# Zero matmuls and doubled scores in the opening of a fused attention and MLP kernel

## The chip, the cores and the metric

The kernel runs on one core of one Trainium2 chip. The metric is the device time of one execution in microseconds (us), as the median of several runs; lower is better. Five engines run their own instruction queues in order and meet at semaphores: TensorE (matmuls and weight loads), VectorE, ScalarE, GpSimd (here also issuing transfers) and SyncE (issuing transfers). A profile is one execution recorded by the hardware profiler, with times counted from the start of its span.

## What is computed

The inputs are q, k and v of 8 batches, 12 heads, 448 positions and 64 numbers per head, and two weight matrices (768 x 2048 and 2048 x 768), all float32. In the reference:

```
scores = (1/sqrt(64)) * q @ k^T              # per batch and head
attn   = max(scores, 0)**2 / 448
x      = attn @ v                            # rearranged to 3584 tokens x 768
h      = x @ w_in
g      = h * sigmoid(1.702 * h)
out    = g @ w_out                           # 3584 x 768, float32
```

There is no softmax, so scores need no row maximum or sum: each tile of scores is cut at zero, squared and multiplied with v.

## The kernel before

**Units.** The attention is cut into 24 units ("quads"), each four heads of one batch, three units to a batch. In a unit the 448 positions are taken as 7 blocks of 64. For each block j the function `scores` (L136) issues four matmuls of 64 x 64 weights by 448 columns, one in each quarter of the array, into one tile `sc` of two memory banks of the accumulator. `relu2` (L150) cuts a tile at zero into `rl` (float16), on ScalarE (L157) or, for a few, on VectorE (L154); a multiplication of `rl` with itself on VectorE then gives `at` (L171 and, here, out of a list of pending ones). When all seven blocks of a unit have their squares, `av_mm` (L174) multiplies them with v in 28 matmuls, and `xt_evac` copies the result to `xt`, the transposed input of the MLP.

**Buffers.** Score tiles share three buffers (`ps_s`), also used by the value products of all units but the first; a score therefore waits for the relu of the score three tiles earlier. All other products share two buffers (`ps_m`). There are three `rl` tiles, so a relu waits for the square three tiles earlier.

**The opening.** Before anything has been loaded, eight matmuls of a tile of zeros with itself (`zero`, L490 to L494) run into a scratch bank. The q and k of units 0 to 5 are loaded with a conversion to float16 by GpSimd's queue and transposed on TensorE: `trans_pe` (L124) issues 14 transposes into one bank, and VectorE copies them to kT or qT (L133). Those of units 6 to 23 are loaded by SyncE's queue, cast (`cast`, L96) and transposed by the transfer engines (`trans`, L107).

**Order.** Everything up to unit 8 and the first two groups of MLP columns is issued in an order written out by hand, a string of words (L521 to L536). `s2.3` is the score of unit 2, block 3 (with `d`: relu on VectorE; with `h`: relu held until the next MLP step), `k3` and `q3` are transposes, `a1` the value product of unit 1 with its copy, `f` and `F` steps of the first MLP product for groups 0 and 1, `m` and `n` of the second, `l` a bundle of loads, `L`, `W`, `K`, `Q`, `R` loads, casts and transposes of later units, other capitals sums of weights. In the kernel before, `e2` squares pending tiles, oldest first, until two are left. As engines keep the order in which they are given their work, a word sets what it is queued behind. After the words a loop mixes MLP steps and visits to the remaining units; after each visit `prefetch` (L599) brings up loads, casts and transposes of later units.

Of the kernel before, what the change touches and what calls it, by code (L numbers as in the profile page):

```python
# [8 lines left out]
F32 = mybir.dt.float32  # L9
F16 = mybir.dt.float16  # L10
AF = mybir.ActivationFunctionType
ALU = mybir.AluOpType
# [3 lines left out]
def kernel(  # L16
# [9 lines left out]
    nc = tc.nc  # L26
# [3 lines left out]
    J = S // 64  # L30
    NP = H // 4
    NU = B * NP
# [26 lines left out]
    ps_s = ctx.enter_context(tc.tile_pool(name="ps_s", bufs=3, space=bass.MemoryType.PSUM))  # L59
# [14 lines left out]
    def quad(t, b, pr):  # L74
        return t[b].rearrange("(a i s) (p j) d -> i (s p) a (j d)", a=2, i=NP, j=J)[pr]

    def load_qk(u):
        b, pr = divmod(u, NP)
        st = units.setdefault(u, {})
        for n, t in (("k", k), ("q", q)):  # L80
            x = stp.tile([128, 2, S], F32, name=f"{n}st", tag=f"{n}st")
            nc.sync.dma_start(
                out=x,
                in_=quad(t, b, pr))
            st[n] = x

    def load_v(u):
        b, pr = divmod(u, NP)
        st = units.setdefault(u, {})
        x = v16p.tile([128, 2, S], F16, name="v16", tag="v16")  # L90
        nc.gpsimd.dma_start(  # L91
            out=x,
            in_=quad(v, b, pr))
        st["v16"] = x
# [20 lines left out]
    def load16(u, n):  # L115
        b, pr = divmod(u, NP)
        st = units.setdefault(u, {})
        x = c16.tile([128, 2, J, D], F16, name=f"{n}16", tag=f"{n}16")
        nc.gpsimd.dma_start(
            out=x,  # L120
            in_=quad({"k": k, "q": q}[n], b, pr))
        st[n + "16"] = x
# [10 lines left out]
        nc.vector.tensor_copy(out=t, in_=ps[:, 0:J * 128])  # L133
        st[n + "T"] = t

    def scores(u, j):  # L136
        st = units[u]
        sc = ps_s.tile([128, 2, 512], F32, name="sc", tag="sc")
        for s in range(2):
            for a in range(2):  # L140
                r = slice(64 * a, 64 * a + 64)
                c = slice(64 * s, 64 * s + 64)
                nc.tensor.matmul(  # L143
                    out=sc[c, a, 0:S],
                    lhsT=st["kT"][r, j, c],
                    rhs=st["qT"][r, :, c],
                    start=True, stop=True)
        return sc

    def relu2(u, j, sc, dve=False):  # L150
        rl = rlp.tile([128, 2, S], F16, name="rl", tag="rl")
        at = atp.tile([128, 2, S], F16, name="at", tag="at")
        if dve:
            nc.vector.tensor_scalar(out=rl, in0=sc[:, :, 0:S], scalar1=0.0, scalar2=None,  # L154
                                    op0=ALU.max)
        else:
            nc.scalar.activation(out=rl, in_=sc[:, :, 0:S], func=AF.Relu)  # L157
        if defer[0]:
            pend.append((at, rl))
        else:  # L160
            nc.vector.tensor_tensor(out=at, in0=rl, in1=rl, op=ALU.mult)
        return at


    defer = [False]
    pend = []

    def flush(n=99):
        while pend and n:
            at, rl = pend.pop(0)  # L170
            nc.vector.tensor_tensor(out=at, in0=rl, in1=rl, op=ALU.mult)  # L171
            n -= 1

# [52 lines left out]
    ats = {}  # L226
# [115 lines left out]
    def weight_sum(o, x, y, op, i, eng):  # L342
        c = slice(2 * i, 2 * i + 2)
        eng.tensor_tensor(out=o[:, c, :], in0=x[:, c, :], in1=y[:, c, :], op=op)
# [110 lines left out]
    def w1(i):  # L455
        for a in range(2):
            nc.gpsimd.dma_start(
                out=win[i][64 * a:64 * a + 64, :, :],
                in_=w_rows[a, :, :, i * WQ * 128:(i + 1) * WQ * 128])
# [26 lines left out]
    with tc.manual_schedule():  # L486
# [3 lines left out]
        zero = gfp.tile([128, 1024], F16, name="zero", tag="gf")  # L490
# [19 lines left out]
        for n in ("k", "q"):  # L510
# [8 lines left out]

        defer[0] = True  # L520
        words = (  # L521
            "e2 e1 s0.0 s0.1 e0 q1 s0.2 e1 s0.3 s0.4 k1 e2 e2 s0.5 k2 e0 e0 s0.6 s1.0 a0m "
            "s1.1 e0 s1.2 e0 q2 s1.3 l0 e1 s1.4 s1.5 e2 s1.6 e1 e1 l1 s2.0 s2.1 e1 e1 e0 e1 "
            "a1 e0 k3 s2.2 s2.3 e1 e0 q3 s2.4 s2.5 e2 e3 e2 e1 s2.6 e1 s3.0 l2 e1 l3 e3 e0 a2 "
            "k4 s3.1 f0 s3.2 e2 e1 e0 e0 s3.3d f1 e1 s3.4h e2 e0 l4 s3.5 f2 q4 e1 e0 e2 f3 e1 "
            "f4 e0 e2 s3.6d e3 e1 e0 s4.0 k5 f5 G1 e2 s4.1 e1 e1 e0 e1 e0 e2 a3 e2 s4.2 f6 e1 "
            "e2 e0 e0 e0 s4.3d e1 e3 e0 l5 s4.4 e2 e1 q5 e2 s4.5d e0 f7 e0 e2 f8 s4.6 s5.0 f9 "
            "s5.1 a4 e2 e2 s5.2 e2 e1 e0 e0 f10 e0 e2 s5.3d e3 l6 f11 f12 L6 L7 f13 e3 s5.4 "
            "e2 s5.5 s5.6h e1 e2 f14 f15 Q6 e2 K6 R6 e1 a5 e0 e3 e0 L8 e2 m2 e2 m1 e2 F0 B2 "
            "W6 A2 C2 Q7 e1 K7 B1 F1 e1 C0 m0 e3 A1 B3 A0 F2 s6.0d e1 A3 B0 e0 e2 s6.1 R7 K8 "  # L530
            "s6.2h e0 e1 F3 e2 s6.3 W7 e0 L9 e1 s6.4h Q8 e2 F4 e3 e0 e2 C3 W8 e2 F5 R8 L10 E3 "
            "K9 s6.5 e0 s6.6 n0 e3 F6 W9 e1 s7.0d e0 s7.1 e2 E2 e2 e0 e2 F7 s7.2 e2 e2 a6 "
            "s7.3 C1 s7.4d F8 F9 e1 W10 e2 e0 Q9 F10 s7.5d e2 e2 e1 e3 s7.6h e3 e2 e2 e1 s8.0 "
            "e2 R9 e2 e3 e0 n1 e3 s8.1 s8.2 e1 a7 K10 E1 e1 e2 L11 s8.3 e1 E0 e2 e3 e2 F11 n2 "
            "e0 s8.4 e3 e1 e0 e0 e3 s8.5 D0 s8.6h e0 e0 Q10 W11 e2 e0 e0 e1 e2 F12 R10 e2 F13 "
            "D2 e3 e0 e0 e2 F14 D3 e1 D1 e0 F15 e1 W12 e0 e0 L12").split()  # L536
        loads = {"0": lambda: (load16(4, "k"), load16(4, "q"), load_v(4), w1(2)),
                 "1": lambda: (load16(5, "k"), load16(5, "q"), load_v(5)),
                 "2": lambda: w1(3),
# [2 lines left out]
        for w in words:  # L542
            t, w = w[0], w[1:]
            if t == "s":
                where = w[-1] if w[-1] in "dh" else ""
                u, j = (int(x) for x in w.rstrip("dh").split("."))
                sc = scores(u, j)
                if where == "h":
                    held.append((u, j, sc))
                else:  # L550
                    ats[u, j] = relu2(u, j, sc, where == "d")
            elif t in "kq":
                trans_pe(int(w), t)
            elif t == "a":
                u = int(w.rstrip("m"))
                if w[-1] == "m":
                    units[u]["av"] = [ps_m.tile([128, 512], F32, name="avm", tag="mm")
                                      for _ in range(2)]
                while any(p[0] is ats[u, jj] for p in pend for jj in range(J)):
                    flush(1)  # L560
                for jj in range(J):
                    av_mm(u, jj, ats.pop((u, jj)))
                xt_evac(u)
                done_units[0] = u + 1
            elif t == "f":
                m1(0, int(w))
            elif t == "F":
                m1(1, int(w))
            elif t in "mn":
                m2(0, int(w), int(t == "n"))  # L570
            elif t in "BACED":
                o, x, y, op = {"B": (w_b, wout[1][0], wout[1][1], ALU.subtract),
                               "A": (w_a, wout[0][0], wout[1][1], ALU.add),
                               "C": (w_c, wout[0][1], wout[0][0], ALU.subtract),
                               "E": (w_e, wout[0][1], wout[1][1], ALU.add),
                               "D": (w_d, wout[1][0], wout[0][0], ALU.add)}[t]
                weight_sum(o, x, y, op, int(w), nc.vector)
            elif t == "G":
                sp_gate(wout[0][int(w)][0:1, 0, 0:64])
            elif t == "L":  # L580
                load_qk(int(w))
            elif t == "W":
                load_v(int(w))
            elif t == "K":
                cast(int(w), "k", nc.scalar)
            elif t == "Q":
                cast(int(w), "q", nc.gpsimd)
            elif t == "R":
                trans(int(w))
            elif t == "e":  # L590
                flush(max(0, len(pend) - int(w)))
            elif t == "l":
                loads[w]()
        defer[0] = False

        loaded = [2 * NP + 7]
        prepped = [2 * NP + 5]

        def prefetch(upto_load, upto_prep):  # L599
            while loaded[0] < min(NU, upto_load):  # L600
                load_qk(loaded[0])
                load_v(loaded[0])
                loaded[0] += 1
            while prepped[0] < min(NU, upto_prep):
                cast(prepped[0], "k", nc.scalar)
                cast(prepped[0], "q", nc.gpsimd)
                trans(prepped[0])
                prepped[0] += 1

        def step_visit():  # L610
            visit4(visits.pop(0))
# [68 lines left out]
```

## Time and profile before

The time is 394.42 us, the median of three runs (393.89 to 394.83). The profiled execution has a span of 393.0 us and a mean granted TensorE clock of 0.984 of full.

| first 60 us in the profile before | us |
|---|---|
| TensorE busy | 51.04 |
| VectorE busy | 42.16 |
| ScalarE busy | 40.18 |
| GpSimd busy | 31.10 |
| mean TensorE clock | 0.91 of full |
| moved by transfers | 198 GB/s |

A "clock" in the profile is the rate that the hardware granted TensorE, as a share of full speed. "Busy" is the time in which an engine had an instruction under way; matmuls overlap one another, and their ends are modelled. "Idle before" a group is the time that the engine waited for something, and the arrow names what ended the wait. In the order of time, a line holds the start, the length, the engine, the source line, the operation and how many instructions were merged. The chain that ended last is followed back from the last instruction, at each step to whatever released it.

### The profile page before, as it was taken

What the parts mean: (1) busy time and instruction counts of PE and PEld (TensorE: products, weight loads), DVE (VectorE), ACT (ScalarE), POOL (GpSimd) and SP (SyncE); (2) the same over time, 40 slices, a digit from 0 to 9 for tenths busy, and PEclk for the clock granted to TensorE, in tenths of its full rate; (3) what the DMA queues carried; (4) which work ended last, traced back from release to release, by engine and by line L of the source; (5) the groups of instructions that cost most, each with busy time, mean ns of one, the idle gap of its engine ahead of it and who ended that gap; (6) DMA issues with size and microseconds to landing.
All of it is one profiled execution on the core that took longest, in us unless ns stands there. A gap on an engine that the chain in (4) does not pass through costs nothing.

```text
span 393.0 us, 7814 instructions
## 1 busy us (share of the span) xinstructions
PE 374.2 (95%) x3104; PEld 193.5 (49%) x3104; DVE 251.9 (64%) x408; ACT 226.2 (58%) x329; POOL 139.5 (35%) x200
## 2 busy tenths in 40 slices
PE   6869999999999999999999999999999999999993
PEld 2435455444455555444455555445444555554552
DVE  2788965899667675577476768275676667123473
ACT  3777673676676765776675656767675662242200
POOL 8444342644543432242442423342332221232100
PEclk9789999999999999999999999999999999999998
DMA  8999999999955929753397928667342301110333
GB/s 119 197 204 205 191 270 211 191 216 116 251 104 170 189 39 231 178 116 76 71 212 129 175 72 209 166 131 111 39 100 39 82 0 42 40 43 0 81 82 81
DMA packets 65221, 50.85 MB, mean 129 GB/s; under 512 B 35744, under 2 KB 61728, under 8 KB 65184
## 3 DMA queue, kind: packets, MB, share of 16 engines
q1 hardware_dynamic: 47872, 35.70, 39.4%
q0 software_dynamic: 17152, 14.55, 25.4%
q8 instruction: 24, 0.39, 0.4%
q10 hardware_dynamic: 160, 0.10, 0.1%
q14 instruction: 13, 0.11, 0.1%
HBM read 45.61 MB, written 11.01 MB: 144 GB/s over the span
## 4 chain that ended last, share of the span: by engine, by line
PE 78%; DVE 7%; ACT 7%; issue 4%; DMA 2%; POOL 1%; ACTq 0%; POOLq 0%
PE ht L292 32%; PE op L359 26%; PE sc L143 8%; PE av L183 7%; PE op L320 4%; ACT rl L157 4%; DVE osb L370 3%; DVE at L171 2%; DMA q<-in_q_dram 1%; ACT k L102 1%; ACT gf L297 1%; PE tr L129 1%; DMA out_dram<-osb 1%; DVE xt L203 0%; ACT eb L368 0%
## 5 line engine op out<-in xcount | busy, mean ns | idle before, releaser
L157 ACT ACTIVATE rl<-sc 128x896 f16<-128x896 f32 x159 | 140.7, 921 | 41.0 <-PE sc L143 40.0
L292 PE MATMUL ht<-xt,win 128*128 128x384 f16 (+1 forms) x768 | 160.8, 353 | 1.8 <-ACT gf L297 1.3
L299 POOL TENSOR_SCALAR gt<-gf 128x384 f16<-128x384 f32 (+1 forms) x128 | 86.1, 673 | 209.2 <-ACT gf L297 208.4
L171 DVE TENSOR_TENSOR at<-rl 128x896 f16<-128x896 f16 x168 | 113.2, 698 | 22.3 <-ACT rl L157 22.0
L297 ACT ACTIVATE gf<-ht 128x384 f32<-128x384 f32 (+1 forms) x128 | 70.1, 548 | 93.4 <-PE ht L292 84.3
L292 PEld LDWEIGHTS <-win 128*128 128x128 f16 x768 | 72.0, 98 | 76.8 <-issue 15.8
L359 PEld LDWEIGHTS <-gt 128*128 128x128 f16 x408 | 39.0, 98 | 32.1 <-issue 6.0
L143 PE MATMUL sc<-qT,kT 64*64 64x448 f16 x672 | 49.7, 366 | 3.8 <-ACT rl L157 2.3
L359 PEld LDWEIGHTS <-as 128*128 128x128 f16 x312 | 30.0, 98 | 23.7 <-issue 3.9
L359 PE MATMUL op<-wsum,gt 128*128 128x384 f16 x224 | 40.7, 326 | 0.5 <-ACT ea L368 0.4
L359 PE MATMUL op<-wout,as 128*128 128x384 f16 x224 | 40.7, 326 | 0.3
L370 DVE SCALAR_TENSOR_TENSOR osb<-op,osb 128x384 f32<-128x384 f32 (+1 forms) x45 | 23.6, 545 | 27.1 <-PE op L359 26.9
L203 DVE CAST xt<-av 128x896 f16<-128x896 f32 (+2 forms) x34 | 25.8, 785 | 19.2 <-PE av L183 19.2
L183 PE MATMUL av<-at,v 64*64 64x448 f16 x644 | 36.2, 359 | 0.7 <-ACT rl L157 0.4
L359 PE MATMUL op<-wout,gt 128*128 128x384 f16 (+1 forms) x184 | 32.4, 319 | 1.6 <-DVE osb L370 0.9
L143 PEld LDWEIGHTS <-kT 64*64 64x64 f16 x672 | 17.2, 106 | 29.4 <-issue 22.3
L370 DVE SCALAR_TENSOR_TENSOR osb<-op,ea 128x384 f32<-128x384 f32 x22 | 12.1, 552 | 24.7 <-PE op L359 13.4
L183 PEld LDWEIGHTS <-v 64*64 64x64 f16 x672 | 20.9, 110 | 14.0 <-issue 3.9
L354 DVE TENSOR_TENSOR as<-gt 128x1024 f16<-128x1024 f16 x36 | 27.1, 779 | 0.0
L91 POOL DMA_DIRECT2D v<-in_v_dram x24 | 17.9, 746 | 9.0 <-PE sc L143 5.2
L104 POOL CAST q<-qst 128x896 f16<-128x896 f32 x18 | 17.2, 954 | 0.3
L102 ACT ACTIVATE k<-kst 128x896 f16<-128x896 f32 x18 | 17.2, 958 | 0.0
(36 smaller groups left out, 158.7 us busy)
## 6 DMA issues: line engine op xcount, KB each, us to landing
out_dram<-osb SPq DMA_DIRECT2D x54, 192.0 KB, 3.0
kst<-in_k_dram SPq DMA_DIRECT2D x18, 448.0 KB, 4.6
qst<-in_q_dram SPq DMA_DIRECT2D x18, 448.0 KB, 5.8
v<-in_v_dram POOLq DMA_DIRECT2D x24, 224.0 KB, 4.5
win<-in_moe_w_in_dram POOLq DMA_DIRECT2D x8, 384.0 KB, 11.9
wout<-in_moe_w_out_dram POOLq DMA_DIRECT2D x4, 768.0 KB, 11.8
k<-in_k_dram POOLq DMA_DIRECT2D x6, 224.0 KB, 8.9
q<-in_q_dram POOLq DMA_DIRECT2D x6, 224.0 KB, 8.9
```

The costliest lines, as they stand in the source:

```text
L102: eng.activation(out=o, in_=i, func=AF.Copy)
L143: nc.tensor.matmul(out=sc[c, a, 0:S], lhsT=st["kT"][r, j, c], rhs=st["qT"][r, :, c], start=True, stop=True)
L157: nc.scalar.activation(out=rl, in_=sc[:, :, 0:S], func=AF.Relu)
L171: nc.vector.tensor_tensor(out=at, in0=rl, in1=rl, op=ALU.mult)
L183: nc.tensor.matmul(out=st["av"][s][64 * a:64 * a + 64, 0:S], lhsT=st["v16"][r, a, 64 * j:64 * j + 64], rhs=at[r, a, :], start=(j == 0), st ...
L203: nc.vector.tensor_copy(out=xts[g][:, 2 * pr:2 * pr + 2, c], in_=st["pair"][:, :, f])
L292: nc.tensor.matmul(out=ht[:, 0:n], lhsT=w[:, kk, fo:fo + 128], rhs=xts[g][:, kk, 0:n], start=(kk == 0), stop=(kk == NK - 1))
L297: nc.scalar.activation(out=gf[:, 0:n], in_=ht[:, 0:n], func=AF.Gelu_apprx_sigmoid, scale=1.0 / SC)
L299: nc.gpsimd.tensor_scalar(out=gts[g][:, f, 0:n], in0=gf[:, 0:n], scalar1=SC, scalar2=1.0, op0=ALU.mult, op1=ALU.mult)
L354: nc.vector.tensor_tensor(out=out_, in0=x, in1=y, op=op)
L359: nc.tensor.matmul(out=op[:, 0:cw], lhsT=lhs[:, f, :], rhs=w[:, f, c0:c0 + cw], start=(start and f == 0), stop=(stop and f == HF - 1))
L370: nc.vector.scalar_tensor_tensor(out=o, in0=op[:, 0:w], scalar=sc, in1=add, op0=ALU.mult, op1=ALU.add)
```

## The change

Three things are added and one is moved.

- A word `z3` issues three matmuls of zeros (128 x 128 by 512 columns) into a score tile taken from its pool ahead of time; the next score then uses that tile. It stands once ahead of `s0.0`, the first score, and once after `q1`, ahead of `s0.2`.
- A flag `t` on a score word issues the four matmuls of the score twice, with the same result. It stands on `s2.0` to `s2.5`, the first six scores of the third quad.
- In `prefetch` the casts and transposes of a unit are issued ahead of the loads of a later one, not after them.
- The words `e` that counted pending squares are replaced by words `x` that name them (`x2.3`); pending squares are kept by name. The order of the squares among the other words is the same.

What the zeros and the doubled scores are for is TensorE's activity: they give it work without use in places where it would wait, so that its clock may stay up. The order of the other instructions on TensorE is unchanged.

```diff
-    def scores(u, j):
+    early = []
+
+    def scores(u, j, times=1):
         st = units[u]
-        sc = ps_s.tile([128, 2, 512], F32, name="sc", tag="sc")
-        for s in range(2):
+        sc = early.pop() if early else ps_s.tile([128, 2, 512], F32, name="sc", tag="sc")
+        for s in [0, 1] * times:
             for a in range(2):
...
-            "e2 e1 s0.0 s0.1 e0 q1 s0.2 e1 s0.3 s0.4 k1 e2 e2 s0.5 k2 e0 e0 s0.6 s1.0 a0m "
...
+            "z3 s0.0 s0.1 x0.0 x0.1 q1 z3 s0.2 s0.3 s0.4 k1 x0.2 s0.5 k2 x0.3 x0.4 x0.5 s0.6 "
+            "s1.0 x0.6 a0m s1.1 x1.0 x1.1 s1.2 x1.2 q2 s1.3 l0 s1.4 s1.5 x1.3 s1.6 x1.4 x1.5 "
+            "l1 s2.0t s2.1t x1.6 x2.0 x2.1 a1 k3 s2.2t s2.3t x2.2 x2.3 q3 s2.4t s2.5t x2.4 "
+            "s2.6 x2.5 s3.0 l2 x2.6 l3 x3.0 a2 k4 s3.1 f0 s3.2 x3.1 x3.2 s3.3d f1 s3.4h x3.3 "
...
-                sc = scores(u, j)
-                if where == "h":
+                sc = scores(u, j, 2 if "t" in where else 1)
+                if "h" in where:
...
-            elif t == "e":
-                flush(max(0, len(pend) - int(w)))
+            elif t == "x":
+                at, rl = pend.pop(tuple(int(x) for x in w.split(".")))
+                nc.vector.tensor_tensor(out=at, in0=rl, in1=rl, op=ALU.mult)
+            elif t == "z":
+                early.append(ps_s.tile([128, 2, 512], F32, name="sc", tag="sc"))
+                for _ in range(int(w)):
+                    nc.tensor.matmul(out=early[0][:, 0, :], lhsT=zero[:, 0:128],
+                                     rhs=zero[:, 0:512], start=True, stop=True)
...
         def prefetch(upto_load, upto_prep):
-            while loaded[0] < min(NU, upto_load):
-                load_qk(loaded[0])
-                load_v(loaded[0])
-                loaded[0] += 1
             while prepped[0] < min(NU, upto_prep):
                 cast(prepped[0], "k", nc.scalar)
                 cast(prepped[0], "q", nc.gpsimd)
                 trans(prepped[0])
                 prepped[0] += 1
+            while loaded[0] < min(NU, upto_load):
+                load_qk(loaded[0])
+                load_v(loaded[0])
+                loaded[0] += 1
```

## The prediction

> **What bounds the kernel now.** I read the page first, then the chain that ended last, then TensorE's order of time in the first 33 us, then a table of stretches cut where the clock changes.
>
> ```profile
> PE 374.2 (95%) x3104; PEld 193.5 (49%) x3104; DVE 251.9 (64%) x408; ACT 226.2 (58%) x329; POOL 139.5 (35%) x200
> ...
> PEclk9789999999999999999999999999999999999998
> ```
>
> TensorE is busy 95% of the span, and its clock is below full in only three places: slices 2 and 3 (10 to 29 us), and the end. From 60 to 360 us it idles 3.7 us in 300 (busy 59.55, 59.49, 58.90, 59.08 and 59.24 of 60 us each), and none of its waits there is for a transfer. A saving at the start should therefore move everything after it. The start is where TensorE is not full: 51.04 of the first 60 us. The chain there, in order of time:
>
> ```profile
> 4.12 5.05 DMA q<-in_q_dram
> 9.17 0.04 issue
> 9.21 0.96 PE tr L129 x14
> 10.17 1.26 PE sc L143 x11
> 11.44 0.89 PE tr L129 x14
> 12.32 0.52 PE sc L143 x4
> 12.84 0.91 PE tr L129 x14
> 13.75 0.02 issue
> 13.77 0.62 DVE kT L133
> 14.40 2.21 DVE at L171 x4
> ...
> 22.71 2.85 PE av L183 x28
> ```
>
> So the chain runs through TensorE from 9.21 to 13.75, then VectorE and ScalarE, then TensorE again in 22.71 to 25.56. Both TensorE pieces run at half clock:
>
> ```profile
> 5.10:8.51 3.41, 1.74 (x36) 1.08 (x36) 1.25 (x2) 0.41 (x1) 3.41 (x6) 1.00 1.22 184
> 8.51:11.92 3.41, 2.71 (x38) 1.64 (x40) 1.78 (x3) 2.49 (x4) 2.59 (x4) 0.50 1.18 180
> 11.92:15.33 3.41, 3.41 (x46) 1.95 (x46) 2.72 (x5) 2.58 (x4) 2.14 (x4) 0.50 1.25 201
> 15.33:18.75 3.42, 2.20 (x46) 1.15 (x38) 2.95 (x8) 2.89 (x4) 0.92 (x2) 1.00 1.24 197
> 18.75:22.16 3.41, 1.92 (x31) 0.84 (x27) 3.17 (x7) 3.10 (x5) 1.88 (x3) 1.00 1.25 201
> 22.16:25.57 3.41, 2.98 (x34) 1.44 (x31) 2.22 (x4) 2.12 (x3) 1.37 (x2) 0.50 1.24 205
> 25.57:28.99 3.42, 2.60 (x48) 1.27 (x48) 3.10 (x6) 2.54 (x4) 1.41 (x2) 1.00 1.27 205
> ```
>
> The first column after the length is TensorE's busy time, the last but two its clock. The clock changes only at multiples of 3.41 us[...]. At full clock, 1.74 and 1.92 us of busy time (51% and 56%) were followed by half; 2.20 and 2.60 us (64%, 76%) were not. At half clock 2.71 us (79%) was not enough to come back; 3.41 and 2.98 us (100%, 87%) were.
>
> [...] 25.57 to 28.99 keeps its clock with only 1.51 us (44%) without its transposes (1.09), while 18.75 to 22.16 loses it with 1.72 us (1.92 less 0.20). I go by total busy time. [...] (weight loads of the warm-up on zeros start 0.43 us apart: 2.05, 2.48, 2.90); no row here shows 512 columns at full clock[...].
>
> **The change, part by part.**
>
> *Zeros before the first scores.* [...] They follow the transposes of q0, issued by 6.88; s0.0 starts at 7.67 after 0.72 us of waiting for the copy of qT. They need only the zero tile and an unused score buffer. They end near 7.55: hidden, cost 0 (at most 0.1). In the window 5.10 to 8.51 busy time goes from 1.74 to 2.39 us (70%), above the 64% that kept its clock: no fall at 8.51.
>
> *Zeros after the transposes of q1.* By the instruction order they stand behind those transposes, ahead of s0.2, not in the 0.97 us in which the transposes wait for q1. So 0.65 us lies on the chain if the clock is full, 3 x 0.427 = 1.28 us if it is half. Queued behind them are s0.2 to s0.4, for which ScalarE already waits 0.92 us at 10.74. Their use is the window 8.51 to 11.92: at full clock the real work in it shrinks to about 1.85 us (54%, a fall at 11.92); with zeros it is 2.5 us (73%).
>
> *The first half-clock stretch, walked forward.* q1 lands at 9.19 (issued 4.12, 5.1 to landing) in both kernels. Transposes at full clock take 0.52 to the next instruction (18.36 to 18.88), zeros 0.65: s0.2 starts at 10.36 against 10.10, its relu at 10.79 (0.43 after the score, as 8.10 after 7.67) against 10.74. Nothing is won so far. Relus follow at 0.81 (4.97 us for six). Three score groups of 0.19 end at 10.94, transposes of k1 at 11.46; s0.5 needs the buffer of s0.2's relu, 11.75; transposes of k2 (landed 5.54 + 6.3 = 11.84) from 11.94 to 12.46; kT's copy ends near 13.05 (before: 14.3). Now the relus need not wait for the squares: s0.3 to s0.6 start at 11.60, 12.41, 13.22, 14.03, the last against 15.02. Its square ends near 15.6, and the last group of the first value product starts at 15.63 against 16.65. Gain 1.0 us, zeros paid for.
>
> *Scores made twice* (s2.0 to s2.5). Six extra groups of 0.19 us (three of 0.38 show the pipeline's tail; 12 matmuls in 0.76 give 0.19 each), 0.37 at half clock. Of s2.0 and s2.1 nothing lies on the path: TensorE waits 0.42 us for ScalarE's buffers before each of their kind. The four of s2.2 to s2.5 stand ahead of the transposes of q3 and of s2.6; the latter waits 0.42 and s3.0 0.81 us for others, so I charge 0.4 us, bounds 0 and 4 x 0.37 = 1.5. Their aim is 18.75 to 22.16, which fell with 1.92. Plus 2 x 0.19 it is 2.30 (67%), enough if nothing else moved. But all arrives 1.0 us earlier, so the window sees what lay at 19.77 to 23.18: three groups of 0.38, 0.47 of the value product, and the extra 0.38, some 2.0 us (58%), between 56% (fell) and 64% (stayed). If the fall stays away, 28 value matmuls take about 1.45 (1.49 at 41.70) in place of 2.83: 1.4 us more.
>
> *The rest.* The new words name each square where a count stood; VectorE's order is the same, cost 0. In the later prefetch the casts and transposes are issued ahead of the loads, both waiting for the same casts as before; TensorE waits there for neither, so 0, at most 0.2 either way.
>
> **A ceiling.** Transfers run without a break (1.22 to 1.27 of 2.00 us per 2 us, about 200 GB/s). k4 is issued at 15.83 and lands 13.3 later, at 29.1; its transposes start at 31.63. So the start can't move by more than 2.5 us. K6's cast at 60.00 follows loads issued at 50.95 and landing in 7.1 at most, 58.0: 2 us of slack.
>
> **Rivals and their times**, from 394.42:
> - A, the forecast: first stretch goes, second stays wholly or partly. 1.0 less 0 to 0.4 for the doubled scores, and in executions whose windows lie otherwise a part of the 1.4: about 1.1 us, 393.3. For: the 70% and 73%. Against: one window position is known.
> - B: both go. 1.0 + 1.4 - 0.2 = 2.2 us, 392.2, under the ceiling.
> - C, no change: the walk's 1.0 is taken by doubled scores (0.4 to 0.75) and by a wait that moves to k2 or k4: 394.2.
> - D, slower: windows lie so that the first zeros straddle a boundary and the fall comes anyway. Second zeros then cost 1.28 on the chain: 395.7; with doubled scores half exposed up to 396.5. For: before's own runs spread 393.89 to 394.83, as they would if windows lay differently. Against: 0.65 us added to a window wherever it falls can only raise its share.
>
> **How the numbers follow.** A 0.42, B 0.25, C 0.19, D 0.14. The likeliest is A: 393.3. About a fifth of A lies within 0.2% (0.79 us) of no change: faster 0.60, same 0.26, slower 0.14. The range reaches over B (392.2 less 0.5 for the ceiling, 391.7) and takes in C and a slight loss, 395.0, leaving out most of D.
>
> **What would show it.** Right: full clock from 8.51 to 15.33 in the profile after; relu of s0.2 near 10.8 as before, the last group of the first value product near 15.6, k4's transposes near 30.5 (A) or 29.2 (B). Wrong: a half-clock stretch while the second zeros run; relus after 10.8 still broken up by waits for squares; TensorE idling before k2's or k4's transposes for a transfer; new waits after 33 us that give the gain back.

## The result, and the profile after

The changed kernel takes 392.72 us (median of four executions, 392.31 to 393.14) against 394.42: a ratio of 0.9958 with a 95% interval of 0.9940 to 0.9975, 1.70 us less. Beside later experiments it was run 22 times more: 392.88 against 394.23, ratio 0.9974 (0.9961 to 0.9987), 1.36 us less by the medians and 0.89 by the means. The larger set is the better estimate of its size.

The page of the profile after, TensorE's row and its granted clock in 40 slices:

```profile
PE 375.0 (96%) x3134; PEld 193.6 (49%) x3134; DVE 247.3 (63%) x408; ACT 226.1 (58%) x329; POOL 138.6 (35%) x200
...
PEclk9999999999999999999999999999999999999998
```

No slice ahead of the end is below full any more. But TensorE's order of time (start, length, operation, idle time before it) shows that this is not the story that the prediction told. First, lines of the profile before:

```profile
5.26 0.58 PE L129 MATMUL tr<-ident,k 128*64 128x128 f16 x14 [0.44 <-DMA k<-in_k_dram]
...
7.67 0.57 PE L143 MATMUL sc<-qT,kT 64*64 64x448 f16 x8 [0.72 <-DVE qT L133]
...
16.65 0.38 PE L183 MATMUL avm<-at,v 64*64 64x448 f16 x4 [0.22 <-DVE at L171]
...
22.71 2.83 PE L183 MATMUL av<-at,v 64*64 64x448 f16 x28 [0.43 <-ACT rl L157]
...
31.63 0.58 PE L129 MATMUL tr<-ident,k 128*64 128x128 f16 x14
```

And of the profile after:

```profile
5.16 0.96 PE L129 MATMUL tr<-ident,k 128*64 128x128 f16 x14 [0.34 <-DMA k<-in_k_dram]
6.27 0.96 PE L129 MATMUL tr<-ident,q 128*64 128x128 f16 x14 [0.15 <-DMA q<-in_q_dram]
7.16 1.46 PE L594 MATMUL sc<-zero 128*128 128x512 f16 x3
8.55 0.96 PE L145 MATMUL sc<-qT,kT 64*64 64x448 f16 x8
9.44 0.76 PE L129 MATMUL tr<-ident,q 128*64 128x128 f16 x14
10.13 0.82 PE L594 MATMUL sc<-zero 128*128 128x512 f16 x3
10.88 0.76 PE L145 MATMUL sc<-qT,kT 64*64 64x448 f16 x12
...
16.35 0.38 PE L185 MATMUL avm<-at,v 64*64 64x448 f16 x4 [0.22 <-DVE at L590]
...
22.41 1.52 PE L185 MATMUL av<-at,v 64*64 64x448 f16 x28 [0.24 <-ACT rl L159]
23.85 0.58 PE L129 MATMUL tr<-ident,k 128*64 128x128 f16 x14
...
30.17 0.58 PE L129 MATMUL tr<-ident,k 128*64 128x128 f16 x14
```

Fourteen transposes take 0.96 us here at 5.16 and 6.27, where before they took 0.58. In the profile before they took 0.96 us at 9.21, where the clock column says 0.50, and 0.58 at 18.36, where it says 1.00. So this execution is at half clock until the middle of the transposes of q1, although the column says 1.00 there. In these traces the record of the clock begins with its first change (5.10 us before, 9.84 after), and what lies ahead of that is shown as full; the profile before, too, shows 1.00 during its eight opening matmuls of zeros, which start 0.43 us apart, where those at full clock in the profile after (10.13, 10.36, 10.57) start 0.23 and 0.22 us apart. The first zeros take 1.46 us and put the first score off from 7.67 to 8.55. Even so the last group of the first value product starts 0.30 us earlier than before (16.35 against 16.65). The second value product, at full clock, then gains most: it takes 1.52 us in place of 2.83. The transposes of k4 start at 30.17 against 31.63, 1.46 us earlier, and the span ends 1.6 us earlier (391.4 against 393.0).

From there to the end nothing was lost. From 60 to 360 us TensorE is busy 296.40 us (59.66 + 59.50 + 58.91 + 59.08 + 59.25), before 296.26.

### The profile page after: what moved, and what is told of

Read it like the earlier page. It is cut to its first block, busy times and chain, and to the rows that moved or that the text cites. A ratio compares the mean times of both kernels' runs of the same rounds, so it can differ in the third digit from the quotient of the medians.

```text
span 391.4 us, 7859 instructions
## 1 busy us (share of the span) xinstructions
PE 375.0 (96%) x3134; PEld 193.6 (49%) x3134; DVE 247.3 (63%) x408; ACT 226.1 (58%) x329; POOL 138.6 (35%) x200
## 4 chain that ended last, share of the span: by engine, by line
PE 78%; DVE 9%; ACT 7%; issue 4%; DMA 1%; POOL 0%; ACTq 0%; POOLq 0%
PE ht L294 32%; PE op L361 26%; PE sc L145 8%; PE av L185 7%; ACT rl L159 4%; PE op L322 4%; DVE osb L372 3%; DVE at L590 3%; ACT k L102 1%; ACT gf L299 1%; DMA q<-in_q_dram 1%; PE tr L129 1%; DVE at L173 1%; PE sc L594 1%; DVE xt L205 0%
## 5 line engine op out<-in xcount | busy, mean ns | idle before, releaser
L301 POOL TENSOR_SCALAR gt<-gf 128x384 f16<-128x384 f32 (+1 forms) x128 | 84.9, 663 | 212.7 <-ACT gf L299 211.6
L173 DVE TENSOR_TENSOR at<-rl 128x896 f16<-128x896 f16 x105 | 67.8, 672 | 16.4 <-ACT rl L159 16.4
L590 DVE TENSOR_TENSOR at<-rl 128x896 f16<-128x896 f16 x63 | 41.6, 683 | 8.1 <-ACT rl L159 7.9
L185 PE MATMUL av<-at,v 64*64 64x448 f16 x644 | 34.8, 350 | 0.5 <-ACT rl L159 0.2
L185 PEld LDWEIGHTS <-v 64*64 64x64 f16 x672 | 20.1, 107 | 13.3 <-issue 3.5
L356 DVE TENSOR_TENSOR as<-gt 128x1024 f16<-128x1024 f16 x36 | 26.3, 756 | 0.0
```

The lines of the kernel that those rows point to most:

```text
L185: nc.tensor.matmul(out=st["av"][s][64 * a:64 * a + 64, 0:S], lhsT=st["v16"][r, a, 64 * j:64 * j + 64], rhs=at[r, a, :], start=(j == 0), st ...
L301: nc.gpsimd.tensor_scalar(out=gts[g][:, f, 0:n], in0=gf[:, 0:n], scalar1=SC, scalar2=1.0, op0=ALU.mult, op1=ALU.mult)
L356: nc.vector.tensor_tensor(out=out_, in0=x, in1=y, op=op)
```

## The experiments

Each variant ran 11 to 22 times, and the kernel before 55 to 75 times beside each set of four. The table gives the difference from the kernel before in its own set, by mean (with the standard error of the variant's mean) and by median, the ratio with its interval, and the mean granted clock, whose stretch ahead of the first change counts as full. The clock of the kernel before was 0.9887 to 0.9898. The new prefetch alone, both groups of zeros, the first group and the doubled scores form the first set, on another chip than the other two sets; rows of different sets can be compared only by their differences from the kernel before.

```
variant                                mean, us       median  ratio (95%)             clock
new prefetch alone                     0.00 +- 0.19   +0.03   0.9999 (0.9986-1.0013)  0.9882
both groups of zeros                  -0.18 +- 0.23   -0.44   0.9993 (0.9976-1.0010)  0.9931
first group of zeros                  -0.26 +- 0.23   -0.45   0.9999 (0.9981-1.0016)  0.9932
transposes in place of zeros          -0.47 +- 0.13   -0.65   0.9987 (0.9976-0.9999)  0.9933
zeros in waits                        -0.02 +- 0.10   -0.30   0.9993 (0.9983-1.0004)  0.9901
doubled scores                        -0.53 +- 0.17   -0.84   0.9984 (0.9970-0.9998)  0.9917
zeros and doubled scores              -0.83 +- 0.16   -1.22   0.9979 (0.9967-0.9992)  0.9955
first zeros and doubled scores        -0.66 +- 0.19   -0.73   0.9984 (0.9972-0.9996)  0.9940
the change                            -0.89 +- 0.17   -1.36   0.9974 (0.9961-0.9987)  0.9950
the change, all scores doubled        -0.99 +- 0.10   -1.37   0.9977 (0.9967-0.9986)  0.9970
doubled scores in waits               -1.11 +- 0.19   -1.42   0.9969 (0.9951-0.9987)  0.9932
zeros and doubled scores in waits     -1.53 +- 0.14   -1.95   0.9961 (0.9949-0.9973)  0.9964
```

### The parts, one by one

Prefetch alone: the words of the change without `z3` and without `t`.

```diff
-            "z3 s0.0 s0.1 x0.0 x0.1 q1 z3 s0.2 ...
+            "s0.0 s0.1 x0.0 x0.1 q1 s0.2 ...
-            "l1 s2.0t s2.1t ...
+            "l1 s2.0 s2.1 ...
```

> The kernel before with casts and transposes ahead of loads in prefetch, nothing else. Clock theory (the gain is half-clock windows that no longer happen in the first 33 us): within 0.3 us of before, mean clock as before, 0.984 to 0.990. Order theory (the later prefetch gives the gain): 1.0 to 1.7 us faster, with TensorE's waits after 60 us shorter.

The ratio is 0.9999: the order theory falls. Its profile gives more than its time, since up to 33 us its work is that of the kernel before, yet its clock changes at other times. The transposes of q1 take 0.60 us in place of 0.96, those of k1 at 10.93 take 0.96 as before, and the two scores at 13.14 are back at 0.57, where before they took 0.96 at 13.66:

```profile
9.14 0.60 PE L129 MATMUL tr<-ident,q 128*64 128x128 f16 x14 [0.96 <-DMA q<-in_q_dram]
...
22.18 1.52 PE L185 MATMUL av<-at,v 64*64 64x448 f16 x28 [0.43 <-ACT rl L159]
...
29.76 0.58 PE L129 MATMUL tr<-ident,k 128*64 128x128 f16 x14
```

The second value product is at full clock without any added work, and the transposes of k4 start at 29.76, 1.87 us ahead of the profile before, in a span of 390.9 us. So the same instructions give both ends of the range. What differs is when the clock changes; the transposes of q1, which wait for a transfer in both, start at 9.14 and 9.21 us. The 189 executions of the kernel before in the three sets show it without a profile, time and mean clock being correlated at -0.74:

```
mean clock         executions   median us   lowest to highest
below 0.9875           64         394.50    393.95 to 395.41
0.9875 to 0.9915       66         394.25    393.00 to 395.33
0.9915 to 0.9955       25         392.80    392.48 to 393.91
above 0.9955           34         393.14    391.82 to 393.53
```

The last row is not the fastest. The mean clock hides half-clock time ahead of the first recorded change. In the profile of the variant called doubled scores in waits, shown further down, 14 transposes still take 0.96 us at 12.43, and yet its mean clock reads 0.998. So the clock column ranks variants only roughly.

Zeros alone, both groups and the first only, and doubled scores alone, each with prefetch as before:

```diff
-            "l1 s2.0t s2.1t x1.6 x2.0 x2.1 a1 k3 s2.2t s2.3t x2.2 x2.3 q3 s2.4t s2.5t x2.4 "
+            "l1 s2.0 s2.1 x1.6 x2.0 x2.1 a1 k3 s2.2 s2.3 x2.2 x2.3 q3 s2.4 s2.5 x2.4 "
```

> The kernel before with both groups of zeros alone. Clock theory: 0.6 to 1.2 us faster, full clock from about 9 to 15 us, a half-clock stretch near 22 to 26 us in most executions. Order theory, and the theory that the doubled scores alone give the gain: 0 to 0.6 us slower, the second zeros being on the chain.

```diff
-            "z3 s0.0 s0.1 x0.0 x0.1 q1 z3 s0.2 s0.3 ...
+            "z3 s0.0 s0.1 x0.0 x0.1 q1 s0.2 s0.3 ...
```

> The kernel before with the zeros ahead of the first scores alone (no zeros after the transposes of q1). Clock theory[...]: the fall moves from 8.5 to about 12 us in some executions; 0.3 to 0.9 us faster, less than both groups together. If the second group only costs its 0.65 us: 0.3 us or more faster than both groups together.

```diff
-            "z3 s0.0 s0.1 x0.0 x0.1 q1 z3 s0.2 s0.3 ...
+            "s0.0 s0.1 x0.0 x0.1 q1 s0.2 s0.3 ...
```

> The kernel before with the first six scores of the third quad made twice, alone. Clock theory: 0.2 to 0.8 us faster, half clock near 9 to 15 us as before, the later half-clock stretch gone in about half the executions. Theory of the doubled scores alone: 1.3 to 1.7 us faster.

Zeros brought less than expected: 0.18 us for both groups and 0.26 for the first alone by the means, both within their errors of nothing, and 0.44 and 0.45 by the medians. Doubled scores brought 0.53, as expected. That is 0.35 more than both groups of zeros with an error of 0.29, so these runs do not rank the two. The two groups of zeros give the same as the first alone: the second group neither costs nor earns anything that these runs can tell.

The profiles show what each part does. With both groups of zeros:

```profile
15.57 0.38 PE L185 MATMUL avm<-at,v 64*64 64x448 f16 x4 [0.26 <-DVE at L590]
...
21.63 2.83 PE L185 MATMUL av<-at,v 64*64 64x448 f16 x28 [0.43 <-ACT rl L159]
...
30.61 0.58 PE L129 MATMUL tr<-ident,k 128*64 128x128 f16 x14
```

With doubled scores:

```profile
12.78 0.96 PE L129 MATMUL tr<-ident,k 128*64 128x128 f16 x14
...
22.71 1.52 PE L185 MATMUL av<-at,v 64*64 64x448 f16 x28 [0.24 <-ACT rl L159]
```

With zeros the clock is full through the first stretch (14 transposes take 0.58 us each time, from 5.11 to 11.98), where the last group of the first value product starts 1.08 us ahead of the profile before, but not in the second: the second value product takes 2.83 us as before. With doubled scores the transposes of k2 take 0.96 us, as before, and the second value product 1.52. The four profiles with zeros, or transposes in their place, and without doubled scores are all of the first kind (k1's transposes 0.58 us, the second value product 2.25 to 2.83), the two with doubled scores and without zeros of the second (0.96 and 1.52). So each part guards its own stretch in these profiles. That the mean gain of the zeros is so much smaller than 1.08 us has a likely reason: the variants are compared with all executions of the kernel before, and only 64 of 189 have a mean clock below 0.9875, as the profile before has (0.984).

### Do they add up?

> Zeros and doubled scores together, with prefetch as before. Theory 1 (the parts help each other: each keeps the clock in one place, and only with both does a whole execution stay at full clock): 1.2 to 1.7 us faster, as the change itself. Theory 2 (the four executions of the change fell on good positions of the clock's windows; the parts add up, 0.2 and 0.5 by their means): 0.6 to 0.9 us faster. Theory 3 (the new prefetch is needed): under 0.5 us faster.

Zeros and doubled scores without the new prefetch gave 0.83 us by the mean; the parts alone sum to 0.18 + 0.53 = 0.71. They add within their errors, and the medians say the same (1.22 against 0.44 + 0.84 = 1.28): theory 2. The two together do not always hold the clock: in this profile the 16 score matmuls from 20.06 us on take 1.77 us, where 16 at full clock take 0.95 (24.44), and the second value product 2.31. The change itself, in 22 executions:

> The changed kernel itself, in many executions. The kernel without the new prefetch gave 0.83 us by the mean and 1.22 by the median of 22 executions. Theory 1 (prefetch does nothing, the first four executions of the change fell on good window positions): 0.7 to 1.3 us faster by the median, mean clock 0.995 to 0.996. Theory 2 (the new prefetch adds to the rest): 1.5 to 1.9 us faster with the same clock.

0.89 by the mean and 1.36 by the median, with a clock of 0.9950: nearest to theory 1, though the median is a little above its range, so the first four executions probably overstated it. Nine of the 22 have a mean clock below 0.995 and took 393.20 to 394.63 us, the other 13 392.13 to 393.40: in a good part of its executions the change does not hold the clock. Its profile is one in which everything that the prediction's walk assumed held, full clock from the transposes of q0 on:

```profile
6.88 0.82 PE L594 MATMUL sc<-zero 128*128 128x512 f16 x3
7.66 0.57 PE L145 MATMUL sc<-qT,kT 64*64 64x448 f16 x8
9.04 0.58 PE L129 MATMUL tr<-ident,q 128*64 128x128 f16 x14 [0.80 <-DMA q<-in_q_dram]
9.55 0.82 PE L594 MATMUL sc<-zero 128*128 128x512 f16 x3
10.30 0.76 PE L145 MATMUL sc<-qT,kT 64*64 64x448 f16 x12
...
15.63 0.38 PE L185 MATMUL avm<-at,v 64*64 64x448 f16 x4 [0.21 <-DVE at L590]
...
21.68 1.52 PE L185 MATMUL av<-at,v 64*64 64x448 f16 x28 [0.24 <-ACT rl L159]
...
29.45 0.58 PE L129 MATMUL tr<-ident,k 128*64 128x128 f16 x14
```

The first score stands where it stood (7.66), the last group of the first value product at 15.63 as walked, k4's transposes at 29.45. This execution was 2.4 us shorter in span than the one profiled before (390.6 against 393.0), close to the 2.2 us of the prediction's case B.

### Where the first stretch's gain goes

Without the second zeros, but with doubled scores:

> Zeros ahead of the first scores and doubled scores, without the zeros after the transposes of q1. If the second zeros keep a window: 0.3 us or more slower than both groups with doubled scores. If the wait for k2 and the squares behind it hides their 0.65 us and nothing else comes of them: within 0.2 us of it.

0.66 against 0.83 by the means, 0.73 against 1.22 by the medians; the difference of the means is within their errors, that of the medians is 0.5. Whether the second zeros earn something beside doubled scores is not settled. The profile shows something else, in the order of time:

```profile
10.88 0.38 PE L145 MATMUL sc<-qT,kT 64*64 64x448 f16 x4
13.18 0.58 PE L129 MATMUL tr<-ident,k 128*64 128x128 f16 x14 [1.92 <-DMA k<-in_k_dram]
```

With a full clock TensorE gets to k2's transposes 1.92 us before k2 has landed. In this profile a long stretch of half clock follows the wait: the transposes of q2 at 18.61 take 0.96 us (0.58 before), the three scores at 19.49 take 1.33 (0.76 before), the second value product at 23.53 takes 2.32, and only k3's transposes at 25.77 are back at 0.58. k4's start at 32.09, 0.46 us later than before. With every score from s1.1 to s3.0 doubled,

> The change, with s1.1 to s1.6, s2.6 and s3.0 made twice as well, so every score from s1.1 to s3.0. Clock theory: after 16 us nearly always at full clock, 1.5 to 2.2 us faster than before unless the doubled scores themselves stand on the path; then no better than the change. Theory that the doubled scores' own time is what limits: 0.3 to 0.8 us slower than the change.

the clock is the highest of all (0.9970) and the time that of the change: doubled scores also stand on the path. From the last group of the first value product to the second value product this profile takes 6.24 us (16.91 to 23.15), that of the change 6.05 (15.63 to 21.68). Here, too, k2 is late:

```profile
11.62 0.38 PE L145 MATMUL sc<-qT,kT 64*64 64x448 f16 x4
13.40 0.58 PE L129 MATMUL tr<-ident,k 128*64 128x128 f16 x14 [1.41 <-DMA k<-in_k_dram]
...
16.91 0.38 PE L185 MATMUL avm<-at,v 64*64 64x448 f16 x4 [0.22 <-DVE at L590]
...
23.15 1.52 PE L185 MATMUL av<-at,v 64*64 64x448 f16 x28 [0.24 <-ACT rl L159]
```

The last group of the first value product starts later than before (16.91 against 16.65), with transposes at 0.58 us from 6.27 on. k2 is issued at 5.54 us in the profiles before and after, and lands 6.3 us later before and 7.3 after; why it varies is not shown. By the profiles' account TensorE waited for it in four of the fourteen, these two and those of transposes in place of zeros (0.78 us) and of zeros in waits (1.24 us), where k2's transposes start at 12.52 to 13.40 us. In the latter two the last group of the first value product starts at 16.02 and 16.07. In the four with zeros, a full clock from the transposes of q0 on (6.21 to 6.47 us) and no wait for k2 it starts at 15.57 to 15.63. So a late k2 takes from 0.4 us up to all of the first stretch's gain in these profiles.

### Activity only where TensorE waits

Two zeros go ahead of q1's transposes, into their wait, in place of three after them; the doubled scores are those that stand ahead of a wait.

```diff
-            "z3 s0.0 s0.1 x0.0 x0.1 q1 z3 s0.2 s0.3 ...
-            "s1.0 x0.6 a0m s1.1 x1.0 x1.1 s1.2 x1.2 q2 s1.3 l0 s1.4 s1.5 x1.3 s1.6 x1.4 x1.5 "
-            "l1 s2.0t s2.1t x1.6 x2.0 x2.1 a1 k3 s2.2t s2.3t x2.2 x2.3 q3 s2.4t s2.5t x2.4 "
-            "s2.6 x2.5 s3.0 ...
+            "z3 s0.0 s0.1 x0.0 x0.1 z2 q1 s0.2 s0.3 ...
+            "s1.0 x0.6 a0m s1.1t x1.0 x1.1 s1.2t x1.2 q2 s1.3 l0 s1.4 s1.5t x1.3 s1.6t x1.4 x1.5 "
+            "l1 s2.0t s2.1t x1.6 x2.0 x2.1 a1 k3 s2.2 s2.3 x2.2 x2.3 q3 s2.4 s2.5 x2.4 "
+            "s2.6 x2.5 s3.0t ...
```

> Zeros ahead of the first scores; two matmuls of zeros ahead of the transposes of q1 (in their wait for the transfer) in place of three after them; doubled scores s1.1, s1.2, s1.5, s1.6, s2.0, s2.1, s3.0, each ahead of a wait of TensorE, in place of s2.0 to s2.5. Clock theory: activity in waits costs nothing and keeps the clock as well: 1.4 to 2.2 us faster than before, at least as good as the change. If what matters is activity just where the change has it: 0.5 to 1.0 us faster.

1.53 us by the mean, 1.95 by the median: the best of all. In its profile this is how doubled scores look when they cost nothing, first in the profile before and then here:

```profile
18.36 0.58 PE L129 MATMUL tr<-ident,q 128*64 128x128 f16 x14 [0.95 <-DVE xt L206]
...
21.09 0.38 PE L143 MATMUL sc<-qT,kT 64*64 64x448 f16 x4 [0.42 <-ACT rl L157]
```

```profile
16.36 0.95 PE L145 MATMUL sc<-qT,kT 64*64 64x448 f16 x16
17.89 0.58 PE L129 MATMUL tr<-ident,q 128*64 128x128 f16 x14 [0.57 <-DVE xt L208]
...
20.61 0.57 PE L145 MATMUL sc<-qT,kT 64*64 64x448 f16 x8 [0.23 <-ACT rl L159]
...
22.23 1.52 PE L185 MATMUL av<-at,v 64*64 64x448 f16 x28 [0.24 <-ACT rl L159]
```

The wait ahead of q2's transposes shrinks from 0.95 to 0.57 us, those behind ScalarE from 0.42 to 0.23: the added groups fill waits and put nothing off, as the steps between these lines are those of before (1.53 against 1.52 us from 16.36, 1.62 against 1.62 from 20.61). One of its 22 executions has a mean clock below 0.995. It ran in another set than the change, so that it beats the change itself by 0.6 us is likely, not shown. Within its own set it is 0.70 +- 0.21 us faster than zeros and doubled scores, and 0.54 +- 0.17 faster than the change with all scores doubled. Its halves, without its zeros and without its doubled scores:

> Doubled scores ahead of waits (s1.1, s1.2, s1.5, s1.6, s2.0, s2.1, s3.0) without any zeros. If the doubled scores placed in waits make the gain of the best version alone: 1.3 us or more faster than before. If zeros and doubled scores each guard one stretch: 0.7 to 1.1 us faster, mean clock near 0.992, a half-clock stretch between 9 and 15 us still in half the executions.

> Zeros in waits (three ahead of the first scores, two ahead of the transposes of q1) without doubled scores. If each guards one stretch: 0.3 to 0.7 us faster than before, mean clock near 0.993. If zeros ahead of q1's transposes cost nothing and zeros after them 0.65 us on the chain: 0.3 us or more faster than both groups as the change has them (0.2 us by the mean).

Doubled scores in waits alone gave 1.11 us by the mean and 1.42 by the median, as much as the whole change. In their profile the first stretch is at half clock, as the second expectation said, with 0.96 us for 14 transposes up to those at 12.43:

```profile
6.29 0.96 PE L129 MATMUL tr<-ident,q 128*64 128x128 f16 x14
7.97 0.96 PE L145 MATMUL sc<-qT,kT 64*64 64x448 f16 x8 [0.72 <-DVE qT L133]
...
12.43 0.96 PE L129 MATMUL tr<-ident,k 128*64 128x128 f16 x14
...
16.30 0.38 PE L185 MATMUL avm<-at,v 64*64 64x448 f16 x4 [0.21 <-DVE at L590]
```

The last group of the first value product starts at 16.30 even so, ahead of the profile before (16.65); q1's transposes start at 8.87 there in place of 9.21. Zeros in waits alone gave nothing (0.02), and both expectations for them fell. In their profile k2's transposes wait 1.24 us for their transfer and the second value product takes 2.25 us, against 1.52 at full clock; whether that is typical of the 14 executions is not known. The two halves sum to 1.13 us against 1.53 together, a difference of 0.4 with an error of about 0.3, so whether they help each other stays open.

### What counts as activity

```diff
-                early.append(ps_s.tile([128, 2, 512], F32, name="sc", tag="sc"))
-                for _ in range(int(w)):
-                    nc.tensor.matmul(out=early[0][:, 0, :], lhsT=zero[:, 0:128],
-                                     rhs=zero[:, 0:512], start=True, stop=True)
+                zt = ps_s.tile([128, 2, 1024], F16, name="zt", tag="sc")
+                for i in range(6 * int(w)):
+                    h = i % 2
+                    nc.tensor.matmul(out=zt[64 * h:64 * h + 64, 0, 128 * (i % 8):128 * (i % 8) + 128],
+                                     lhsT=zero[:, 0:64], rhs=ident[:, :], is_transpose=True)
```

> Both groups of zeros as in the change, without doubled scores and new prefetch, but each group of three matmuls replaced by 18 transposes of zeros with the identity, of about the same length at full clock (18 x 0.037 = 0.66 us). If any busy time of TensorE keeps the clock: mean clock near 0.993, as with zeros. If transposes count little: mean clock 0.989 to 0.990 as before, falls at about 8.5 to 9.5 us as often as before, 0 to 0.5 us slower than before.

The clock is 0.9933, as with zeros (0.9931), against 0.9887 for the kernel before in its set, so transposes keep it too. In the profile one stretch shows it; TensorE's busy time, clock and the rest in it, first of all its instructions, then of the 14-fold transposes, then of the added ones:

```profile
5.29:8.70 3.41, 2.17 (x54) 1.00 1.24 189
```

```profile
5.29:8.70 3.41, 1.09 (x28) 1.25 (x2) 1.00 1.24 189
```

```profile
5.29:8.70 3.41, 0.67 (x18) 1.00 1.24 189
```

Of 2.17 us 1.09 + 0.67 = 1.76 are transposes, and the clock stayed at full past 8.70 (it fell at 22.36). The stretch from 5.10 to 8.51 of the profile before holds the same 28 transposes and 8 score matmuls and differs by the 18 added transposes; after it the clock fell (1.74 us busy, then 0.50). The runs test whether transposes keep a full clock, not whether they alone bring it back.

## Why the prediction was right, and where it was wrong

**Mechanism and time.** The gain is half-clock time that no longer happens in the first 33 us, and it reaches the end undiminished, as forecast. Forecast 1.1 us; measured 1.70 at first, 1.36 (median) and 0.89 (mean) in the larger set. Of the signs named in advance, the last value group near 15.6 and full clock through the first stretch came in the profile of the larger set, not in the profile after, which is at half clock until 9.84 us. One sign of being wrong came too, TensorE idling ahead of k2's transposes for a transfer, in four of the profiles.

**First zeros cost nothing.** Right at full clock (first score at 7.66 against 7.67), wrong at half clock: the first score comes 0.88 us later in the profile after. Not all of it is the zeros: from the transposes of q0 to the first score it takes 2.28 us there (6.27 to 8.55) and 1.68 in the profile of doubled scores in waits, at half clock and without zeros (6.29 to 7.97), so that 0.60 is theirs. The forecast took the clock to be full from 5.10 us on, as in the profile before; in the profile after it is half until 9.84. This half clock ahead of the first recorded change is missing from the forecast's list of the places below full.

**Second zeros, the walk.** Forecast 10.36 for s0.2 and 15.63 for the last value group; 10.30 and 15.63 in the execution at full clock. The forecast's 0.65 us for three zeros at full clock was the author's estimate; half of the 0.43 us that lie between zeros at half clock, times three, gives the same. The zeros at full clock in the profile after start 0.23 and 0.22 us apart, but in both profiles of the change the next score starts 0.75 us after the first of them (9.55 to 10.30, 10.13 to 10.88), not 0.65.

**First stretch worth 1.0 us, second stretch stays (case A).** Case A is what the zeros alone do in their profile: first stretch won by 1.08 us, second at half clock, k4's transposes 1.02 us earlier. The change does not stay there. In its two profiles the second stretch is at full clock too: the one of the larger set is case B in full, the profile after is case B in the second stretch with 0.30 us of the first. The weak step is that one execution stood for all. The walk took k2's landing for fixed at 11.84 us, and transposes that waited for it started as late as 13.40; a "wait that moves to k2" stood only under case C. It also took the clock to be full from 5.10 us on. And the kernel before was taken at its profile's clock, 0.984, while 125 of its 189 executions have a mean clock above 0.9875. That the middle of so wide a spread came near 1.1 us is in part luck: more was won in the second stretch than case A said, and less, on average, in the first.

**Doubled scores charged 0.4 us.** About twice too much, and inside its bounds. At full clock the way from the second value product to k4's transposes takes 7.77 us with s2.2 to s2.5 doubled (21.68 to 29.45 in the change) and 7.58 without (22.18 to 29.76 with the new prefetch alone): 0.19 us. s2.0 and s2.1 cost nothing, as forecast: the second value product starts at 22.71 with doubled scores alone as in the profile before.

**Prefetch 0.** Right, 0.00 +- 0.19.

**56% falls, 64% stays.** Not a sharp line. In the profile after, the stretch from 16.67 to 20.08 keeps its clock with 1.82 us of 3.41 (53%):

```profile
3.01:6.43 3.42, 2.92 (x23) 1.23 (x23) 0.27 (x1) 0.00 (x0) 3.35 (x7) 1.00 1.11 161
6.43:9.84 3.41, 3.41 (x33) 1.42 (x33) 0.98 (x2) 0.65 (x1) 3.35 (x6) 1.00 1.15 172
...
16.67:20.08 3.41, 1.82 (x42) 0.93 (x33) 3.32 (x8) 2.80 (x4) 1.42 (x2) 1.00 1.24 200
```

Tables of such stretches of 3.41 us, between 3.01 and 32.40 us, stand for four profiles: before, after, transposes in place of zeros, and doubled scores in waits. In them the clock fell three times, after stretches in which TensorE was busy 44% (1.50 us, transposes in place of zeros), 51% and 56% (before). The other stretches at full clock were busy 53% (the last line above) and 64% or more, and no fall followed. What decides a fall between 53 and 56% is not shown. For the return, 2.92 us (85%) in the first line was not enough (the durations above show half clock until the end of the second line), nor were 2.90 and 2.69 us (85% and 79%) in doubled scores in waits and 2.71 us (79%) before; 2.98 us (87%) before was, and so was a stretch of 100% in each of the four.

**Slower (case D).** No variant was slower than the kernel before on average. What it feared for the second zeros, that they run at half clock, happened to the first ones in the profile after; it cost 0.60 us there and not the gain.

## What to carry to other kernels

Where TensorE waits in many short pieces, ask whether its granted clock is part of the path. Here it was (the second value product takes 2.83 us at half clock and 1.52 at full), and filling those waits with work of no use paid, best where that work stood directly ahead of a wait (1.53 us by the mean; 0.89 for the change, in another set). Before costing a stretch that runs at half clock, ask what else arrives there: a faster TensorE found a transfer that was not yet in (waits of 0.78 to 1.92 us for k2), and a walk with landing times of one execution does not see that. And with a difference of some 0.3%, measure many executions: one profile shows one set of times at which the clock changes, and four executions probably overstated this change.

## What was not expected of the hardware

- The same kernel took from 391.82 to 395.41 us in 189 executions, and its mean clock goes with it (correlation -0.74).
- The clock fell in the profile before, at 8.51 and 22.16 us, though TensorE was never idle longer than 0.97 us between 5 and 23 us.
- The clock column reads 1.00 ahead of the first recorded change; only durations (0.96 against 0.58 us for 14 transposes) tell that TensorE started at half clock. With doubled scores in waits they still take 0.96 us at 12.43, at a recorded mean of 0.998.
- With the most activity (all scores from s1.1 to s3.0 doubled) the mean clock was the highest, 0.9970, and the time was not the lowest: 392.76 us median, against 392.17 with fewer doubled scores, placed in waits, at 0.9964.
